# A second DRAIN on GpSimd, placed between the output stores of the last two experts

## The chip, the cores and the metric

The kernel runs on one core of one Trainium2 chip. The metric is device time in microseconds for one execution, and the number that counts is the median over several executions. Time before: 370.25 us, median of 3 runs (368.98 to 373.83).

## What is computed

A gated linear attention over 4 batches, 8 heads, 768 steps and head size 48 gives 3072 tokens of width 384. A mixture of 8 experts then takes them: each expert gets exactly 3072 / 8 = 384 tokens by a greedy assignment on the logits, and each token's output row is one expert's two-layer network.

```python
for t in range(S):
    state = alpha[:, :, t, :, None] * state + np.einsum('bhd,bhe->bhde', k[:, :, t], v[:, :, t])
    y[:, :, t] = np.einsum('bhd,bhde->bhe', q[:, :, t], state)
...
logits = x @ w_gate                     # x: the tokens, 3072 x 384
...                                     # greedy choice, 384 tokens to each expert
for e in range(E):
    mask = assigned == e
    h = np.maximum(x[mask] @ w1[e], 0.0)
    out[mask] = h @ w2[e]
```

## The kernel before

The first 100 us or so are the attention, in 24 units of 128 steps. Then the experts follow one another, `i` = 0 to 7. An expert's 384 tokens are three blocks of 128, `b` = 0 to 2 (`NB` = 3), and its hidden width of 1024 is eight blocks of 128, `q` = 0 to 7 (`FB` = 8), whose weights come in four groups `g` (`GP` = 4). For each `q`, `ffn1` makes the hidden block (`h`, then `hh` and `hl`, its rounded part and the rest), and `ffn2` two blocks later adds its share to the three outputs `y`, one PSUM bank for each token block. Numbers are carried as a high and a low part, so each product is three matmuls.

GpSimd (POOL) issues nearly all transfers of this stage: the gather of an expert's tokens (`xr`, line 1125), the loads of its weights (`wset` and `raw`, lines 1164 and 1178), the loads that add the exact weight onto its negated high part (`wset`, line 1208), and the stores of the output (`out_dram`, line 1335). A store is an indirect DMA that scatters 128 rows of 384 numbers to the tokens' places. Ahead of each stands a small MEMSET of `pcol` (line 1334).

The stores are numbered by `c = i * NB + b`, so that store 20 is the last of expert 6, and 21, 22 and 23 are those of expert 7, the last. Store `c` waits for the eviction of its bank from PSUM to `yo` (ScalarE on line 1326, and for store 23 half of it by VectorE on line 1329). For the last expert the last four `q` are worked through one token block after another (`LAST_BLOCKS` = 4), so that its three outputs are ready one after another and not all at the end.

The order on each engine is fixed while the program is built: every piece of work is an `op(engine, duration, function, after=..., at=...)` and `plan` places them by a list schedule with these durations. What really makes an instruction wait on the chip are the semaphores that the framework derives from the tiles, not the durations or `after`.

When all work is placed, the framework ends the program (line 1413): SyncE waits in turn for the last count of each semaphore, then every engine runs a DRAIN and reports, GpSimd collects the reports and releases all, the semaphores are cleared, and a second such round ends the span. At the start of the program (line 1379) there is one round of the same kind. These are the only DRAINs of GpSimd before the change: one at the start, three in the end.

Of the kernel before, what the change touches and what calls it, by code (L numbers as in the profile page):

```python
# [29 lines left out]
SUBS, SINGLES, WHOLE = (1, 1), 2, 0  # L30
HL_Q = ((0,) * 8, (0,) * 8)
BY_DVE = ((0, 1), (0,))
XL_PE = 1
LB = (0.15, 0.4, 0.7)
LC, LX, LR = (0.15, 0.25, 0.4), (0.15, 0.3, 0.6), (0.15, 0.4, 0.5)
FIRST_HI, FIRST_SP = (1, 1, 2), 0
# [6 lines left out]
def gla_moe_kernel(ctx, tc, q, k, v, alpha, w_gate, w12, out):  # L43
# [10 lines left out]
    E = w_gate.shape[1]  # L54
# [145 lines left out]
    def op(eng, dur, fn, r=(), w=(), banks=(), at=0.0, after=(), lat=LAT, take=None, give=None, follow=(), boost=0.0,  # L200
           dma=0.0, soft=(), small=False, shape=None, ahead=0.12,
           clear=None, until=None, again=LAT):
        o = Op()
        o.small, o.shape, o.ahead, o.clear, o.until, o.again = small, shape, ahead, clear, until, again
        o.take, o.give, o.follow, o.boost, o.dma, o.soft = take, give, follow, boost, dma, soft
        o.eng, o.dur, o.fn, o.banks, o.at, o.lat = eng, dur, fn, banks, at, lat
        o.idx = len(ops)
        pre = set(after)
        for key in r:
            pre |= set(lastw[key])  # L210
            users.setdefault(key, []).append(o)
        for key in w:
            nm, ver = key
            old = (nm, ver - RING.get(nm, 1))
            pre |= set(users.get(old, ())) | set(lastw.get(old, ()))
            lastw.setdefault(key, []).append(o)
        o.pre = pre
        ops.append(o)
        return o
# [64 lines left out]
    V, G, A, P_ = nc.vector, nc.gpsimd, nc.scalar, nc.tensor  # L284
# [448 lines left out]
    for n in range(Y_EARLY, Y_IN_ATTENTION):  # L733
        o = sps[n % 2].rearrange("p a b -> p (a b)")
        xo = None
        for h in range(2):
            xo = op("PE", 0.2, shape=128, fn=lambda n=n, h=h, o=o: (turn_out(n, o, 2 * h), turn_out(n, o, 2 * h + 1)),
                    r=[("yt", n)], after=[*lastw["sm", NU - 1], *([xo] if h else [])], banks=(f"S{n % 2}",), at=40.0 + n,
# [6 lines left out]
    for _ in range(FILLS):  # L745
# [4 lines left out]
        after=lastw["sm", NU - 1] + lates, at=40.0)  # L750
# [13 lines left out]
    GP = FB // 2  # L764
# [36 lines left out]
    def start(i):  # L801
        return F0 + TE * i
# [335 lines left out]
    his, accs, late_w = {}, {}, []  # L1138
# [89 lines left out]
    def prep(i):  # L1228
# [3 lines left out]
        for b in range(NB):  # L1232
# [3 lines left out]
            def ob(b=b, own=own):  # L1236
                bank = YB[b] if own else X2 if b == 1 else XB
                return bank[:, :DB * 128].rearrange("p (d t) -> p d t", d=DB)
# [3 lines left out]
            def tr(b=b, ob=ob):  # L1242
                for d in range(DB):
                    P_.matmul(ob()[:, d], XR[r2][:, b, d * 128:(d + 1) * 128], ident, is_transpose=True, start=d == 0,
                              stop=d == DB - 1 and i >= XL_PE, skip_group_check=True)

# [4 lines left out]
                    w=[("xh", i)], at=at, lat=0.1)  # L1251
            if i < XL_PE:
                x = op("PE", 0.2, lambda ob=ob, bs=bs: P_.matmul(
# [14 lines left out]
    def pe(d_, fn, after, at, **kw):  # L1268
        pe_last[0] = op("PE", d_, fn, after=list(after) + ([pe_last[0]] if pe_last[0] else []), at=at, **kw)
        first_pe.append(pe_last[0])  # L1270
        return pe_last[0]
# [32 lines left out]
    def ffn2(i, qs):  # L1304
        for b in range(NB):
            bs = slice(b * 128, (b + 1) * 128)
            for q in qs:
                n_ = i * FB + q
                g = q // 2
                c0 = (2 + q % 2) * Dm  # L1310

                def fn(n, q=q, b=b, bs=bs, g=g, c0=c0, m=n_ % RX):
                    hi, lo = (WS[i % 2][:, j, g, c0:c0 + Dm] for j in range(2))
                    a, w = ((HHT[m], hi), (HHT[m], lo), (HLT[m], hi))[n]
                    P_.matmul(YB[b][:, :Dm], a[:, bs], w, start=q == 0 and n == 0, stop=q == FB - 1 and n == 2)  # L1315

                for n in range(3):
                    y = pe(0.1735, lambda n=n, fn=fn: fn(n), [(his, accs, his)[n][i, g, 1]],
                           start(i) + (q + 2) * TE / FB,
                           r=[("hl" if n == 2 else "hh", n_), ("wl1" if n == 1 else "wh1", i * GP + g)],  # L1320
                           w=[(f"yb{b}", i)] if q == 0 and n == 0 else [], lat=0.25)
            if FB - 1 in qs:
                c = i * NB + b
                at = start(i) + (FB + 2) * TE / FB
                cut = Dm // 2 if c == E * NB - 1 else Dm
                xs_ = [op("ACT", 0.49, lambda b=b, c=c, cut=cut: A.activation(YO[c % 5][:, :cut], YB[b][:, :cut], AF.Copy),  # L1326
                          after=[y], w=[("yo", c)], at=at, boost=25, lat=0.1)]
                if cut < Dm:
                    xs_.append(op("DVE", 0.3, lambda b=b, c=c, cut=cut: V.tensor_copy(YO[c % 5][:, cut:], YB[b][:, cut:Dm]),
                                  after=[y], w=[("yo", c)], at=at))  # L1330
                users.setdefault((f"yb{b}", i), []).extend(xs_)

                def scatter(b=b, c=c):
                    G.memset(pcol, 0.0)
                    st_ = nc.gpsimd.indirect_dma_start(  # L1335
                        out=out, out_offset=bass.IndirectOffsetOnAxis(ap=IDX[i][:, b:b + 1], axis=0),
                        in_=YO[c % 5], in_offset=None)
                    for other in scattered:
                        tc.declare_no_dep(st_.ins, other.ins, reason="every token's row is stored once")
                    scattered.append(st_)  # L1340

                op("POOL", 1.27, scatter, after=xs_, r=[("yo", c)], at=at + 1, dma=1.2)

    x = None
    for n in range(E * FB + 2):
        i, q = divmod(n, FB)
        if i < E:
            if q == 0:
                if i < NR:
                    x = round_(i, x)  # L1350
                else:
                    last(i, *x)
            if i == 0 and q % 2 == 0:
                ffn1(i, q, (0, 1))
                ffn1(i, q + 1, (0, 1))
            ffn1(i, q, (0, 1, 2) if i else (2,))
        if n >= 2:
            i, q = divmod(n - 2, FB)
            if i < E - 1 or q < FB - LAST_BLOCKS:
                ffn2(i, [q])  # L1360
            elif q == FB - 1:
                ffn2(i, list(range(FB - LAST_BLOCKS, FB)))
# [54 lines left out]
```

## Time and profile before

| | |
|---|---|
| median of 3 runs | 370.25 us (368.98 to 373.83) |
| the profiled execution | 369.01 us |
| its span, first to last instruction | 367.4 us |
| TensorE busy | 350.3 us, 95% |
| VectorE busy | 267.0 us, 73% |
| ScalarE busy | 185.8 us, 51% |
| GpSimd busy | 177.9 us, 48% |
| share of software (GpSimd) queue in DMA time | 54.2% of 16 engines' span |

The profiled execution takes 1.6 us more than its span, and is at the lower end of the runs shown. A DRAIN counts as work of an engine's sequencer, not as busy time, so none of it is in the busy shares. Names such as POOLq or SPq are the sequencers of GpSimd and SyncE.

### The profile page before, as it was taken

To read this page: it belongs to the slowest core of one execution; us is meant where nothing else is said; L and a number is where in the kernel's file an instruction comes from. 1 tells how busy PE (TensorE), PEld (TensorE's weight loads), DVE (VectorE), ACT (ScalarE), POOL (GpSimd) and SP (SyncE) were. 2 spreads that over 40 slices of the span, in tenths; PEclk is the share of its full clock that TensorE was granted. 3 is DMA by queue.
4 is the path that set the end of the run, shared out by engine and by line. 5 is a ranking of instruction groups with operands and counts; after the bars stand their busy time and mean duration, and the time that the engine had idled before them with its cause. 6 is when DMAs were issued, how large, how long until landed. Compare 5 with 4: busy or idle time off the path is not lost.

```text
span 367.4 us, 9669 instructions
## 1 busy us (share of the span) xinstructions
PE 350.3 (95%) x3710; PEld 310.8 (85%) x3710; DVE 267.0 (73%) x741; ACT 185.8 (51%) x387; POOL 177.9 (48%) x298
## 2 busy tenths in 40 slices
PE   8989999999999999899999999999999999999990
PEld 4778888887776779789899989889989999999990
DVE  7999999998878998888978978878777733131110
ACT  4697888886551741651552553543462474343120
POOL 2898999999402312351524625603722862304021
PEclk9999999999999999999999999999999999999996
DMA  7999998840176956999799699698898899986001
GB/s 232 368 351 377 394 300 265 272 131 2 45 249 221 324 105 167 306 173 271 245 218 260 206 243 237 206 272 165 277 266 171 297 337 239 287 201 127 24 22 43
DMA packets 28782, 81.71 MB, mean 222 GB/s; under 512 B 3904, under 2 KB 10304, under 8 KB 28736
## 3 DMA queue, kind: packets, MB, share of 16 engines
q0 software_dynamic: 11024, 52.70, 54.2%
q1 hardware_dynamic: 17712, 28.39, 22.7%
q8 instruction: 29, 0.48, 0.5%
q14 instruction: 17, 0.14, 0.1%
HBM read 71.64 MB, written 9.44 MB: 221 GB/s over the span
## 4 chain that ended last, share of the span: by engine, by line
PE 61%; DVE 19%; issue 9%; DMA 3%; POOL 3%; SPq 1%; ACT 1%; POOLq 0%; DVEq 0%; ACTq 0%
PE h L1283 21%; PE y L1315 21%; PE y L541 3%; DVE sc L449 3%; PE xt L882 3%; PE s L495 2%; DVE ga L454 2%; PE h L1135 2%; DVE kh L459 2%; DVE wset L1190 2%; DMA al<-in_alpha_dram 2%; DVE cmp L935 1%; DMA vr<-in_v_dram 1%; POOL out_dram L1335 1%; DVE xl L1259 1%
## 5 line engine op out<-in xcount | busy, mean ns | idle before, releaser
L1315 PE MATMUL y<-wset,hh 128*128 128x384 f32 x384 | 101.7, 342 | 0.0
L1283 PE MATMUL h<-xh,wset 128*128 128x384 f32 x384 | 93.4, 345 | 0.3 <-DVE hl L1298 0.3
L1296 ACT ACTIVATE hh<-h 128x384 fp32r<-128x384 f32 x64 | 31.3, 490 | 93.7 <-PE h L1283 84.3
L1315 PEld LDWEIGHTS y<-wset,hh 128*128 128x128 f32 x384 | 69.2, 188 | 1.0 <-issue 1.0
L1283 PEld LDWEIGHTS h<-xh,wset 128*128 128x128 f32 x384 | 68.1, 188 | 0.8 <-DVE hl L1298 0.6
L1315 PE MATMUL y<-wset,hl 128*128 128x384 f32 x192 | 65.9, 343 | 0.0
L1298 DVE SCALAR_TENSOR_TENSOR hl<-h,hh 128x384 fp32r<-128x384 f32 x64 | 35.3, 554 | 39.6 <-ACT hh L1296 38.9
L1208 POOL DMA_DIRECT2D wset<-in_w_dram x23 | 20.9, 909 | 63.9 <-ACT wset L1204 63.8
L1283 PE MATMUL h<-xl,wset 128*128 128x384 f32 x192 | 47.3, 345 | 0.0
L1335 POOL DMA_INDIRECT out_dram<-yo,idx x24 | 24.9, 1039 | 41.3 <-ACT yo L1326 37.4
L1204 ACT ACTIVATE wset<-wset 128x768 fp32r<-128x768 f32 x46 | 36.6, 840 | 12.6 <-DMA wset<-in_w_dram 12.2
L1125 POOL DMA_INDIRECT xr<-x_dram,idx x24 | 25.4, 1060 | 23.5 <-DVE idx L1121 9.0
L1315 PEld LDWEIGHTS y<-wset,hl 128*128 128x128 f32 x192 | 36.1, 188 | 0.5 <-issue 0.4
L1283 PEld LDWEIGHTS h<-xl,wset 128*128 128x128 f32 x192 | 34.1, 188 | 0.9 <-issue 0.7
L502 POOL TENSOR_SCALAR_AFFINE_SELECT sm<-sm 128x512 f32<-128x512 f32 x48 | 32.2, 693 | 3.2 <-ACT sm L500 2.9
L464 POOL TENSOR_TENSOR qh<-qr,ga 128x512 f32<-128x512 f32 (+1 forms) x25 | 29.8, 1193 | 5.3 <-DVE ga L454 4.3
L454 DVE TENSOR_TENSOR_SCAN ga<-al,d 128x516 f32<-128x516 f32 (+1 forms) x25 | 29.6, 1183 | 1.8
L449 DVE TENSOR_TENSOR_SCAN sc<-al,d 128x516 f32<-128x516 f32 (+1 forms) x25 | 29.3, 1173 | 1.3 <-DMA al<-in_alpha_dram 1.2
L500 ACT ACTIVATE sm<-s 128x512 f32<-128x512 f32 x48 | 26.1, 595 | 7.3 <-PE s L495 6.8
L495 PE MATMUL s<-qh,kh 64*128 64x128 f32 x384 | 27.4, 282 | 1.0 <-POOL qh L464 1.0
L495 PEld LDWEIGHTS s<-qh,kh 64*128 64x128 f32 x384 | 23.6, 189 | 2.4 <-POOL qh L464 2.1
L1178 POOL DMA_DIRECT2D raw<-in_w_dram x9 | 5.2, 580 | 41.4 <-DVE bk L1098 19.0
(218 smaller groups left out, 590.7 us busy)
## 6 DMA issues: line engine op xcount, KB each, us to landing
wset<-in_w_dram POOLq DMA_DIRECT2D x46, 768.0 KB
raw<-in_w_dram POOLq DMA_DIRECT2D x9, 768.0 KB
qr<-in_q_dram SPq DMA_DIRECT2D x24, 256.0 KB, 4.7
kr<-in_k_dram SPq DMA_DIRECT2D x24, 256.0 KB, 4.8
al<-in_alpha_dram SPq DMA_DIRECT2D x23, 258.5 KB, 4.7
vr<-in_v_dram SPq DMA_DIRECT2D x24, 192.0 KB, 4.6
x_dram<-xga SPq DMA_DIRECT2D x8, 384.0 KB, 2.7
x_dram<-xga SPq DMA_DIRECT2D x8, 192.0 KB, 3.3
```

Source lines behind the costliest of these rows:

```text
L449: V.tensor_tensor_scan(sc[:, lo + 1:hi + 1][:, ::-1], a[:, lo + 1:hi + 1][:, ::-1], dps[:, FO + lo:FO + hi][:, ::-1], 1.0, op0=OP.mult, op ...
L454: V.tensor_tensor_scan(ga[:, lo:hi], a[:, lo:hi], dps[:, lo:hi], 1.0, op0=OP.mult, op1=OP.add)
L464: (V if n in Q_DVE else G).tensor_mul(qh[:, ps_], qr[:, ps_], ga[:, lo:hi].rearrange("p (g x) -> p g x", x=C1)[:, :, 1:])
L495: P_.matmul(sps[h][:, p], kh[hs, p], qh[hs, p], start=True, stop=True)
L500: op("ACT", 0.6, lambda h=h: A.activation(sm[:, h], sps[h], AF.Copy), r=[(f"S{h}", n)], w=[("sm", n)], banks=(f"S{h}",), at=n + 0.4)
L502: op("POOL", 0.65, lambda h=h: G.affine_select(sm[:, h], sm[:, h], pattern=[[0, HP], [1, C]], compare_op=OP.is_ge, fill=0.0, base=0, chann ...
L1204: pre.append(op("ACT", 0.84, lambda hs=hs: A.activation(WS[i % 2][:, 1, g][:, hs], WS[i % 2][:, 0, g][:, hs].bitcast(F32), AF.Copy, scale= ...
L1283: P_.matmul(o(), WS[i % 2][:, a, g, c0 + d * 128:c0 + (d + 1) * 128], x[:, d], start=m_ == 0 and d == 0, stop=m_ == 2 and d == DB - 1)
L1296: a_ = op("ACT", 0.49, lambda: A.activation(HHT[m], o(), AF.Relu), after=[y], r=[("hb", n_)], w=[("hh", n_)], at=at, boost=25, lat=0.1)
L1298: op("DVE", 0.474, lambda: V.scalar_tensor_tensor(HLT[m], o(), 0.0, HHT[m], op0=OP.max, op1=OP.subtract), after=[a_], r=[("hb", n_), ("hh" ...
L1315: P_.matmul(YB[b][:, :Dm], a[:, bs], w, start=q == 0 and n == 0, stop=q == FB - 1 and n == 2)
L1335: st_ = nc.gpsimd.indirect_dma_start(out=out, out_offset=bass.IndirectOffsetOnAxis(ap=IDX[i][:, b:b + 1], axis=0), in_=YO[c % 5], in_offse ...
```

## The change

One instruction is added to GpSimd's queue: a DRAIN, directly behind store 20. It stands ahead of the MEMSET of store 21. It waits for no semaphore and raises none, and no other instruction gained or lost a wait. On all five engines the other instructions stand in the same order as before. The duration of 6.0 and the `after` list tell only the planner where to put it: behind store 20 and behind the last adding loads of the last expert's weights, all of which stood ahead of store 20 already.

```diff
-XL_PE = 1
+XL_PE, DRAINED = 1, 20
...
-                op("POOL", 1.27, scatter, after=xs_, r=[("yo", c)], at=at + 1, dma=1.2)
+                stored = op("POOL", 1.27, scatter, after=xs_, r=[("yo", c)], at=at + 1, dma=1.2)
+                if c == DRAINED:
+                    op("POOL", 6.0, lambda: G.drain(), after=[stored, *(accs[E - 1, g, 0] for g in range(GP))], at=at + 2)
```

## Rows read from the trace of the kernel before

**Rows 1.** The page: span; busy time, share and instructions of TensorE.

```profile
span 367.4 us, 9669 instructions
PE 350.3 (95%) x3710; PEld 310.8 (85%) x3710; DVE 267.0 (73%) x741; ACT 185.8 (51%) x387; POOL 177.9 (48%) x298
```

**Rows 2.** Chain that ended last, its last pieces: start us, us, what.

```profile
358.47 1.01 issue
359.47 1.19 POOLq L1413
```

**Rows 3.** Timeline, 352 to 368: start, us, engine, line, operation, [idle before].

```profile
358.33 0.34 PE L1315 MATMUL y<-wset,hl 128*128 128x384 f32 x1
...
359.07 0.36 DVE L1329 COPY yo<-y 128x192 f32<-128x192 f32 x1 [5.53 <-ACT yo L1326]
```

**Rows 4.** Line 1413, 359.4 to 360: duration ns min/median/max, first and last start.

```profile
L1413 DVEq DRAIN  x1: 395/395/395, 359.1 to 359.1; - x1
L1413 POOLq DRAIN  x1: 7103/7103/7103, 359.5 to 359.5; - x1
```

**Rows 5.** Line 1413, 362.2 to 363, SyncE's sequencer.

```profile
L1413 SPq EVENT_SEMAPHORE  x9: 28/28/28, 362.3 to 362.8; - x9
L1413 SPq DRAIN  x2: 7/7/7, 362.9 to 362.9; - x2
```

**Rows 6.** Waits of SyncE from 360.5 on: us in total, times, longest.

```profile
SPq L1413 <- PEq L1413: 4.4, 2, 3.9
SPq L1413 <- DMA out_dram<-yo,idx: 2.3, 1, 2.3
```

**Rows 7.** Line 1413, from 366.6 on, GpSimd's sequencer.

```profile
L1413 POOLq EVENT_SEMAPHORE  x4: 17/17/17, 366.6 to 367.3; - x4
...
L1413 POOLq DRAIN  x2: 46/75/104, 366.8 to 367.1; - x2
```

**Rows 8.** Line 1379, the first us of the program, GpSimd's sequencer.

```profile
L1379 POOLq DRAIN  x1: 184/184/184, 0.5 to 0.5; - x1
```

**Rows 9.** Stretches of the span: busy us (instructions), granted clock, DMA share, GB/s.

```profile
core 0: us, PE busy (x) PEld busy (x) DVE busy (x) ACT busy (x) POOL busy (x), PEclk, DMA share, GB/s
...
360.66:362.30 1.64, 0.00 (x0) 0.00 (x0) 0.00 (x0) 0.00 (x0) 0.01 (x1) 0.50 0.33 120
362.30:366.60 4.30, 0.00 (x0) 0.00 (x0) 0.00 (x0) 0.00 (x0) 0.00 (x0) 0.50 0.00 0
```

**Rows 10.** DMA issues by line and tile: engine, times, KB each; those of GpSimd.

```profile
wset<-in_w_dram POOLq DMA_DIRECT2D x46, 768.0 KB
raw<-in_w_dram POOLq DMA_DIRECT2D x9, 768.0 KB
...
xr<-x_dram,idx POOLq DMA_INDIRECT x24
out_dram<-yo,idx POOLq DMA_INDIRECT x24
...
probe<-in_moe_w_gate_dram,bsel POOLq DMA_INDIRECT x1
```

**Rows 11.** Timeline of GpSimd from 331 on: the last load, stores 18 to 23.

```profile
331.10 0.88 POOL L1208 DMA_DIRECT2D wset<-in_w_dram  x1 [7.39 <-ACT wset L1204]
...
337.76 1.01 POOL L1335 DMA_INDIRECT out_dram<-yo,idx  x1 [0.19 <-issue]
338.77 0.11 POOL L1334 MEMSET pcol<- 128x1 f32 x1
339.07 0.96 POOL L1335 DMA_INDIRECT out_dram<-yo,idx  x1 [0.19 <-issue]
340.02 0.12 POOL L1334 MEMSET pcol<- 128x1 f32 x1
355.31 0.95 POOL L1335 DMA_INDIRECT out_dram<-yo,idx  x1 [15.17 <-ACT yo L1326]
...
357.39 0.96 POOL L1335 DMA_INDIRECT out_dram<-yo,idx  x1 [1.01 <-ACT yo L1326]
...
359.71 0.96 POOL L1335 DMA_INDIRECT out_dram<-yo,idx  x1 [1.24 <-DVE yo L1329]
```

**Rows 12.** Line 1335, the output stores: ns min/median/max, first and last start.

```profile
L1335 POOL DMA_INDIRECT out_dram<-yo,idx x24: 955/1008/1707, 161.9 to 359.7; - x24
```

## Prediction

> **What bounds the kernel now.** I read the page first: TensorE is busy for 350.3 of 367.4 us [rows 1], so the body of the kernel belongs to it, and an instruction on GpSimd can matter only where GpSimd is late or where TensorE has already stopped. The chain that ended last ends on GpSimd's sequencer at the program's closing line, and nothing on it follows [rows 2]. So I read the end in order of time. TensorE's last matmul is over at 358.33 + 0.34 = 358.67, and VectorE's half of the last eviction at 359.07 + 0.36 = 359.43 [rows 3]. The last store is issued from 359.71 to 360.67 [rows 11]. SyncE waits 2.3 us for that store to land, begins the rest of its waits at 362.3, and has done its own drains at 362.9 [rows 5, 6]. Then nothing moves: from 362.30 to 366.60 every engine's busy time is 0.00 and the DMA share is 0.00 [rows 9]. SyncE waits 3.9 us for its release [rows 6]. The row puts that wait down to the sequencer of TensorE, which had long been done. What really is late is GpSimd's DRAIN: it starts at 359.47 and takes 7.10 us, so it ends at 366.57 [rows 2, 4]. The report round starts at 366.6 [rows 7], and the span ends 0.8 us later at 367.4. So the last 3.7 us (366.6 - 362.9) ahead of that round belong to one instruction, the final DRAIN of GpSimd.
>
> **What that DRAIN does.** VectorE's drain ends at 359.1 + 0.4 = 359.5, together with its last instruction at 359.43 [rows 3, 4]. GpSimd's is another matter: it ends 366.57 - 360.67 = 5.90 us after its last issue and 366.57 - 362.3 = 4.27 us after that issue's data has landed [rows 4, 5, 11]. In those 4.27 us no transfer moves, so it isn't waiting for data. It is doing, or waiting for, something of its own. What that grows with can be read from the other three drains of GpSimd. The one at the start, with no transfer issued before it, takes 0.184 us [rows 8]. The two behind the long one, with no transfer in between, take 0.104 and 0.046 us [rows 7]. The long one follows 46 + 9 + 24 + 24 + 1 = 104 transfers that GpSimd has issued since the program began [rows 10]. So a drain's length hangs on transfers that no drain has yet cleared away. Whether it hangs on how many there are, or only on there being any, the trace of before can't show, since there is but one drain with transfers before it.
>
> The two ends of this unknown: if it goes by the number, each of 104 costs 4.27 / 104 = 41 ns to 5.90 / 104 = 57 ns, and a drain behind three transfers has 0.12 to 0.17 us of own work. If it is one fixed job, it takes 4.27 us after the landing however few there are. I take the number. The nearest rows are the stores: they follow each other 337.76, 339.07 on one queue with 0.19 us of idle time between a store and its MEMSET [rows 11], so what one transfer leaves to be done is not of the size of 4 us, or it would have to be put off; a hundred small leftovers put off to the drain add up to it, and one leftover does not. The fixed job stays as a rival.
>
> **The added DRAIN, in its place.** It stands behind store 20, whose issue ends at 339.07 + 0.96 = 340.03 [rows 11]. Ahead of it are 101 of the 104 transfers; the last big one was issued at 331.10 [rows 11]. By the store at the end its data lands 362.3 - 360.67 = 1.6 us after issue, so at 341.6. Then 101 x 41 ns = 4.2 us, or at most 101 x 57 ns = 5.8 us, puts its end between 345.8 and 347.5. Queued behind it are only the MEMSETs and stores 21 to 23 and the program's end, and store 21 can't be issued before its eviction, at 355.31 after 15.17 us of idle time [rows 11]. So 7.8 us of cover remain (355.31 - 347.5), and the added drain costs **nothing**. No engine waits on a semaphore of it. TensorE, VectorE and ScalarE run on as before, since all weights of the last expert are already issued.
>
> If that cover were gone: store 22 has 1.01 us of idle time before it and store 23 has 1.24 us [rows 11], so store 21 could be 1.01 + 1.24 = 2.25 us late before store 23 moved. The drain would have to last until 357.5, that is 17.5 us, 2.5 times the longest one in the trace. From there on each further us costs one us.
>
> **The final DRAIN, after.** It now follows three transfers. It can't end before the last of them is out at 360.67, and if it waits for the landing not before 362.3; with 0.12 to 0.17 us of work it ends at 362.5 at the latest. SyncE's last drain at 362.9 is then later. The report round would start at 362.9 instead of 366.6, so the gain is **3.7 us**: less than the 4.27 us that vanish from the drain, since 0.6 us of SyncE's waits come out from under it. That also bounds the gain from above: a drain of no length at all gives no more, because SyncE sets the end next. From below the bound is 0, for a fixed job.
>
> The sum against the profiled execution: 369.01 + 0 - 3.7 = 365.3 us. The profiled one is at the low end of the runs shown, and their median is 1.2 us above it. I name 365.7, between the sum and the sum with that distance.
>
> **A rule weighed against the trace.** The drain's end at 366.57 stands 4.27 us behind the last landing, with no engine busy in between [rows 4, 5, 9]. The Trainium skill, page "PSUM — Partial Sum Buffer", section "Engine vs sequencer instructions", says that a drain waits for its engine to go fully idle. Taken by itself that rule speaks against this change, since the last store is the same before and after: by it the sum would be 369.0 in place of 365.3. The trace agrees for VectorE; for GpSimd it leaves 4.27 us that the rule doesn't explain.
>
> **Rivals.**
> *One fixed job (no change).* The final drain pays 4.27 us after the landing whenever any transfer came before it. For it: a single long drain can't tell. Against it: the stores' spacing, as above. The added drain is covered all the same, so the time is 369.0, at the runs' median 370.25. Chance 0.14. A relative of it: the work of a drain has to be fetched before it runs, and the stores in between drive it out again. The Trainium skill, page "GPSIMD Engine Reference", section "Instruction dispatch", has some 6 us (5.95) for the first call of newly loaded code, with no instruction to be seen in the profile; the 5.90 us here is close to it, and no run here shows whether that is more than chance.
> *Only what is still running (no change).* The 4.27 us are the completion of the last store alone, in a form that the trace doesn't show; an earlier drain then takes nothing from it. For it: the drain's end is the only sign of when GpSimd is done. Against it: the store's count has reached SyncE by 362.3 and the DMA share is 0.00 from there on [rows 5, 9]. The time is again 369.0. Chance 0.06. It is what the rule of "PSUM — Partial Sum Buffer" in the Trainium skill would make of this kernel.
> *In part.* The work goes with something of which the last three stores hold a larger share than 3 in 104 (rows, or time since the transfer), and the final drain ends between 362.9 and 366.57. Halfway gives 367.2. Chance 0.06.
> *Slower.* The added drain outlasts its cover, say because each earlier transfer costs more than the final drain shows. Place: the gap ahead of store 21. It decides from 17.5 us on; at 20 us the last store is 2.5 us late. Then the time is 369.01 + 2.5 = 371.5 if the final drain keeps its length, 367.8 if it doesn't. Also under this: the first store after the drain is dearer. The dearest store in the trace takes 1.707 us against a median of 1.008 [rows 12], and 0.7 us more disappears in the 1.01 us of idle time before store 22. Chance 0.03.
> *The forecast:* 0.71.
>
> **How the numbers follow.** Predicted 365.7. The forecast's own range is 364.6 (0.7 below the sum, since executions differ by tenths and nothing in the rows gives more than 3.7) to 366.9 (1.6 above the sum). The partial case and the near part of the two no-change cases reach up to 369.5; what lies beyond it, their rest and the slower case, is about 0.15. So 364.6 to 369.5. About 2%, 7.4 us, is what a measurement of this kernel can tell from no change. The whole gain is half of that, so it should come out as within 2%: 0.93. Faster by over 2% needs a gain of twice what the end of the program holds, or scatter of the runs on top: 0.05. Slower by over 2% needs an added drain of 17.5 + 7.4 = 24.9 us: 0.02.
>
> **What would show each step.** A DRAIN of POOLq on a new line starts near 340.0 and lasts 5.8 to 7.5 us: the leftover goes by number and lies under cover. Store 21 still starts near 355.3: cover holds. The first of the closing drains of POOLq falls from 7.10 to about 3 us (ending with the landing) or 1.4 us (not waiting for it), SyncE's longest wait at the closing line falls from 3.9 us to about 0.2, and the span becomes 363.7. Wrong, by the fixed job: the closing drain still takes about 7.1 us although the added one took as long. Wrong, by the slower rival: store 21 waits for the drain and not for its eviction. A short added drain, under 2 us, with a long final one would say that neither number nor presence of earlier transfers is what it pays for.

## The result, and the profile after

The changed kernel takes 366.34 us (median of 6 runs, 364.96 to 367.59); the kernel before, measured beside it, 370.08 us (6 runs, 368.98 to 373.83). The medians differ by 3.7 us. The ratio is 0.9892, with a 95% interval of 0.9856 to 0.9929, which is 4.0 us less, between 2.6 and 5.3. So the gain is within 2%, and it is clear of no change.

The page of the changed kernel has one instruction more, and a body that is no shorter; TensorE's busy time is 351.0 us, against 350.3 [rows 1].

```profile
span 365.6 us, 9670 instructions
PE 351.0 (96%) x3710; PEld 311.3 (85%) x3710; DVE 267.6 (73%) x741; ACT 185.9 (51%) x387; POOL 178.3 (49%) x298
```

The sequencers' instructions on the new line (1344) and on the closing line (now 1415), with their least, median and longest duration in ns and the start of the first and the last:

```profile
L1344 POOLq DRAIN  x1: 7667/7667/7667, 340.0 to 340.0; - x1
...
L1415 POOLq DRAIN  x3: 46/104/2963, 361.4 to 365.3; - x3
L1415 SPq DRAIN  x3: 7/7/7, 364.7 to 365.1; - x3
```

The added DRAIN lasts 7.67 us, and the first closing one has gone from 7.10 to 2.96 us [rows 4]. SyncE's waits at the closing line, in total, times and longest:

```profile
SPq L1415 <- PEq L1415: 0.7, 2, 0.5
```

It was 4.4 us, 3.9 the longest [rows 6]. The 0.5 us that is now the longest is the second of the two waits, which before was 4.4 - 3.9 = 0.5 as well; the first is down to 0.2. The timeline of GpSimd, with idle time in brackets, answers to [rows 11]:

```profile
339.66 1.01 POOL L1335 DMA_INDIRECT out_dram<-yo,idx  x1 [0.18 <-issue]
340.67 0.11 POOL L1334 MEMSET pcol<- 128x1 f32 x1
340.98 0.96 POOL L1335 DMA_INDIRECT out_dram<-yo,idx  x1 [0.19 <-issue]
347.78 0.10 POOL L1334 MEMSET pcol<- 128x1 f32 x1 [5.84 <-issue]
357.21 0.95 POOL L1335 DMA_INDIRECT out_dram<-yo,idx  x1 [9.34 <-ACT yo L1326]
358.16 0.12 POOL L1334 MEMSET pcol<- 128x1 f32 x1
359.29 0.96 POOL L1335 DMA_INDIRECT out_dram<-yo,idx  x1 [1.01 <-ACT yo L1326]
360.25 0.11 POOL L1334 MEMSET pcol<- 128x1 f32 x1
361.61 0.96 POOL L1335 DMA_INDIRECT out_dram<-yo,idx  x1 [1.24 <-DVE yo L1329]
```

The MEMSET of store 21 now waits 5.84 us behind the drain, and store 21 still waits for its eviction, with 9.34 us to spare. Stores 22 and 23 follow as before, with the same 1.01 and 1.24 us of idle time.

The span of this execution is only 1.8 us shorter (365.6 against 367.4), though the end of the program, from the end of the last issue, has gone from 367.4 - 360.67 = 6.7 us to 365.6 - 362.57 = 3.0 us. The difference of 1.9 us was there before the drain was reached: store 19 starts at 339.66 where it started at 337.76 [rows 11]. Executions of one kernel differ by that much: the spans of the six timed ones run from 363.3 to 365.9 us.

### The profile page after: what moved, and what is told of

The parts are those of the page before. It is cut to its first block, busy times and chain, and to the rows that moved or that the text cites. A ratio compares the mean times of both kernels' runs of the same rounds, so it can differ in the third digit from the quotient of the medians.

```text
span 365.6 us, 9670 instructions
## 1 busy us (share of the span) xinstructions
PE 351.0 (96%) x3710; PEld 311.3 (85%) x3710; DVE 267.6 (73%) x741; ACT 185.9 (51%) x387; POOL 178.3 (49%) x298
## 4 chain that ended last, share of the span: by engine, by line
PE 50%; DVE 18%; issue 13%; DMA 10%; POOL 5%; ACT 2%; POOLq 1%; SPq 1%; DVEq 0%; ACTq 0%
PE h L1283 16%; PE y L1315 16%; DMA wset<-in_w_dram 5%; PE y L541 3%; DVE sc L449 3%; PE s L495 3%; DVE ga L454 3%; DVE kh L459 2%; DMA raw<-in_w_dram 2%; PE xt L882 2%; DMA al<-in_alpha_dram 2%; DVE wset L1190 1%; POOL out_dram L1335 1%; PE xt L1244 1%; PE h L1135 1%
```

## Experiments

The kernels stand on the kernel before, and only the last on the changed one. A DRAIN behind a store is put in by hand inside `scatter`, unseen by the planner, so that the order of all other work stays as it was. What is compared is the drains themselves and the end of the program, since the rest varies by some 2 us from one execution to the next. Landings are the last of the 16 counts that a store adds to its semaphore in the trace.

**One drain early, behind store 2.**

```diff
                     scattered.append(st_)
+                    if c == 2:
+                        G.drain()
```

> The added DRAIN stands behind store 2 (end of expert 0) and nowhere else; 23 transfers ahead of it, 81 behind it. By number of transfers (57 ns each, counted from the end of the last issue): the added drain has 1.3 us of work, less than the 1.6 us its last store needs to land, so it ends 1.6 to 1.9 us behind that issue; the final drain ends 81 x 57 ns = 4.6 us behind the last issue (before: 5.9), and the end of the program, from the last issue to the span's end, is 5.4 us (before 6.7, changed kernel 3.0). Once only (the first drain behind any transfer pays some 5.8 us, later ones find it done): the added drain takes 5.8 us, the final one ends about 1.8 us behind the last issue, the end of the program is 3.0 us.

The added DRAIN and the closing ones:

```profile
L1342 POOLq DRAIN  x1: 11751/11751/11751, 163.7 to 163.7; - x1
...
L1415 POOLq DRAIN  x3: 52/104/7883, 366.3 to 374.7; - x3
```

"Once only" is out: the final drain is 7.88 us long, although one with 23 transfers went before. But the count as I had it is wrong in two ways. The final drain ends 5.09 us behind the last landing, where 81 transfers at 41 ns give 3.3, and 6.69 us behind the last issue, where 57 ns give 4.6. And the added drain lasts 11.75 us and ends 9.9 us behind the issue of store 2, where 1.6 to 1.9 was expected. The stretch from the store's issue to its landing, in busy time, clock, DMA share and GB/s, shows why:

```profile
164.70:174.40 9.70, 9.70 (x73) 9.07 (x72) 8.13 (x36) 1.48 (x3) 0.87 (x1) 1.00 0.81 195
174.40:175.40 1.00, 1.00 (x18) 0.84 (x16) 0.41 (x4) 0.00 (x0) 0.00 (x0) 1.00 0.00 0
```

Store 2 lands only at 174.4, 8.9 us behind its issue, in a stretch in which the DMA engines are 81% busy: the two loads of weights issued just ahead of the stores, at 159.29 and 160.78, land at 169.3 and 173.0. The drain waits for store 2, and then works 1.0 us more. So a drain of GpSimd waits for all that GpSimd has in flight. Meanwhile nothing else can be issued from GpSimd's queue:

```profile
176.75 0.57 POOL L1178 DMA_DIRECT2D raw<-in_w_dram  x1 [11.18 <-DVE nd L964]
```

In the kernel before this load is issued at 169.78. Here it starts 1.3 us behind the end of the drain (175.43), which is what it waited for, and not the instruction of VectorE that the row names. The weights of a later expert come 7.0 us late, and the last store is issued at 367.48 instead of 360.67. One execution took 376.63 us.

**Three drains, behind stores 2, 11 and 20.** The same edit with `if c in (2, 11, 20)`.

> Three added DRAINs, behind stores 2, 11 and 20, with 23, 40 and 38 transfers between them and 3 behind the last. By number: 1.3, 2.3 and 2.2 us of work, so they end 1.6 to 1.9, 2.3 and 2.2 us behind the issue ahead of each (together about 6 us where the changed kernel's one drain has 5.8); the final one ends with the landing, 1.8 us behind the last issue. Once only: 5.8 us for the first, about 1.8 us for the second, third and last. One fixed job per drain: about 5.8 us for each of the four.

```profile
L1342 POOLq DRAIN  x3: 5094/6535/11107, 162.8 to 347.4; - x3
...
L1415 POOLq DRAIN  x3: 46/104/2950, 368.8 to 372.7; - x3
```

From the landing ahead of each, the three work 0.99 us (23 transfers), 1.69 us (40) and 1.60 us (38), and the final one 0.16 us (3). That is neither one fixed job nor one paid once: it is the number, at 41 ns each, counted from the landing and not from the issue. The 57 ns of the prediction's other end would be 2.3 and 2.2 us from the issue; they are 4.60 and 3.21. The end of the program is 3.04 us long, as in the changed kernel, but the first two drains have no cover, and the last issue ends at 369.96. One execution took 374.61 us.

**A drain before any transfer.** In the kernel before, at the end of the attention:

```diff
+    def first_transfer():
+        G.drain()
+        nc.gpsimd.indirect_dma_start(out=probe, ...)
-    op("POOL", 1.2, lambda: nc.gpsimd.indirect_dma_start(
+    op("POOL", 1.2, first_transfer, ...)
```

> The kernel before with one DRAIN ahead of GpSimd's very first transfer, behind all of its work in the attention. By number of transfers: that drain takes under 0.4 us, the final one again 5.9 us behind the last issue, the time that of before. By number of GpSimd's instructions of all kinds (298, so 20 ns each): that drain takes about 3.5 us beyond the end of the work ahead of it, and the final one ends some 2.3 us behind the last issue. A first call that has to be fetched: several us here, and the final one as long as it likes.

The drain, and from the timeline GpSimd's last work ahead of it:

```profile
L749 POOLq DRAIN  x1: 897/897/897, 94.5 to 94.5; - x1
```

```profile
94.02 1.27 POOL L502 TENSOR_SCALAR_AFFINE_SELECT sm<-sm 128x512 f32<-128x512 f32 x2 [0.32 <-ACT sm L500]
```

It lasts 0.90 us, more than the 0.4 that were expected, because its record starts while the work ahead of it still runs. It ends at 94.48 + 0.90 = 95.37, 0.08 us behind that work (95.29). GpSimd's instructions as such leave nothing to a drain, nor does the first drain in the body cost a fetch of several us. The final one is again 7.10 us long and ends 4.30 us behind the landing. One execution took 368.82 us.

**24 small transfers more.** The kernel before, with 24 loads of 32 bytes behind the first transfer:

```diff
+    tiny = [rw.tile([1, E], F32, name=f"tiny{j}") for j in range(24)]
...
+        for t in tiny:
+            nc.gpsimd.dma_start(t, w_gate[:1])
```

> The kernel before, no added DRAIN, with 24 more transfers of 32 bytes each behind GpSimd's first transfer, in the gap between the attention and the experts (their data is not used). By number: 128 transfers x 57 ns = 7.3 us from the last issue to the end of the final drain (before 5.9), the end of the program 8.1 us, the time 1.4 us above before. By rows or bytes: 24 x 1 row on top of 104 x 128 rows, so 5.9 us and the time of before.

```profile
L1419 POOLq DRAIN  x3: 46/110/8086, 360.9 to 369.5; - x3
```

The final drain is 8.09 us long, 0.98 us more, and ends 5.28 us behind the landing. 0.98 / 24 = 41 ns for a transfer of one row and 32 bytes, the same as for the 104 others (4.30 / 104), most of which are far larger. Number counts, rows and bytes don't. The end of the program is 7.7 us, not 8.1: the 57 ns were too high. One execution took 371.37 us.

**Behind store 2 once more, and behind store 11.** The kernel of the first run again, and `if c == 11`.

> The kernel of the first of these runs once more (one added DRAIN, behind store 2), since its final drain was longer than the rest of the runs would have it: 5.09 us behind the last landing for 81 transfers, where 23, 38, 40, 101, 104 and 128 transfers all fit 0.05 us + 41 ns each. By that line: 3.4 us behind the last landing. If something of the order of transfers since a drain counts beside their number: again 5.1 us.

> One added DRAIN, behind store 11, with 63 transfers ahead of it and 41 behind. By 0.05 us + 41 ns for each transfer, counted from the last landing: the added drain ends 2.6 us behind the landing of store 11, the final one 1.7 us behind that of store 23. If the final drain after an early one is dearer (as behind store 2, with a surplus of 1.7 us): 2.5 us or more for the final one. Once only: final 0.2 us.

```profile
L1415 POOLq DRAIN  x3: 52/104/7885, 366.7 to 375.1; - x3
```

The surplus behind store 2 comes back to the hundredth: 5.09 us behind the landing for 81 transfers. With the drain behind store 11, the added one takes 2.63 us behind the landing, as expected (2.6), and the final one 1.82 us, 0.09 above the 1.73 that 0.05 us + 41 ns each would give. One execution each took 377.04 and 373.43 us.

**Where the surplus comes from: behind the first transfer, store 5 and store 8.** The edits `if c == 5` and `if c == 8`, and a drain right behind the first transfer of all.

> One added DRAIN right behind GpSimd's very first transfer, in the gap between the attention and the experts: 1 transfer ahead of it, 103 behind it. By 0.05 us + 41 ns each: it ends 0.1 us behind the landing of that transfer, and the final drain 4.3 us behind the last landing, so the time is that of before. If in a later batch the transfers beyond the 40th cost twice as much (which would fit 5.09 us for 81 and 1.82 us for 41): 4.3 + 63 x 41 ns = 6.9 us behind the last landing, 2.6 us slower than before. If any earlier drain makes the final one 1.7 us dearer: 6.0 us.

> One added DRAIN, behind store 5 (end of expert 1): 36 transfers ahead of it, 68 behind. It waits for store 5 to land and then works 1.5 us. The final drain, behind the last landing: 2.8 us by the number alone; 4.0 us if those beyond the 40th of a later batch cost twice as much; 4.5 us if an earlier drain costs 1.7 us.

> One added DRAIN, behind store 8 (end of expert 2): 50 transfers ahead of it, 54 behind. It waits for store 8 to land and then works 2.1 us. The final drain, behind the last landing: 2.3 us by the number alone; 2.8 us if those beyond the 40th of a later batch cost twice as much; 4.0 us if an earlier drain costs 1.7 us.

One execution each took 370.57, 376.78 and 375.86 us. The drains that had transfers to clear away (left out are nine that repeat a row within 0.01 us, or 102 transfers with 4.22), with the time from the last landing to their end, and what 0.05 us + 41 ns for each transfer gives:

| kernel | transfers since the drain before | behind the landing, us | line, us |
|---|---|---|---|
| first transfer: added | 1 | 0.09 | 0.09 |
| store 22: final | 1 | 0.09 | 0.09 |
| changed: final | 3 | 0.17 | 0.17 |
| store 2: added | 23 | 0.99 | 0.99 |
| store 5: added | 36 | 1.53 | 1.53 |
| three drains: third | 38 | 1.60 | 1.61 |
| three drains: second | 40 | 1.69 | 1.69 |
| store 8: added | 50 | 2.10 | 2.10 |
| store 11: added | 63 | 2.63 | 2.63 |
| changed: added | 101 | 4.18 | 4.19 |
| store 22: added | 103 | 4.26 | 4.27 |
| before: final | 104 | 4.30 | 4.31 |
| 24 small: final | 128 | 5.28 | 5.30 |
| first transfer: final | 103 | 4.26 | 4.27 |
| store 11: final | 41 | 1.82 | 1.73 |
| store 8: final | 54 | 2.89 | 2.26 |
| store 5: final | 68 | 4.02 | 2.84 |
| store 2: final | 81 | 5.09 | 3.37 |

Fourteen rows lie on the line within 0.02 us. The line was drawn after those of 3, 23, 38, 40, 101, 104 and 128 transfers; those of 1, 36, 50, 63 and 103 were measured afterwards. The last four lie above it by 0.09, 0.63, 1.18 and 1.72 us, in steps of about 41 ns for each transfer beyond the 39th or 40th. "Any earlier drain makes the final one 1.7 us dearer" is out by the first three of them. "Those beyond the 40th of a later batch cost twice" fits all four (2.8 and 4.0 were expected for stores 8 and 5), and falls with the drain behind the first transfer, whose later batch of 103 has no surplus. The two batches always add up to 104, so the surplus of the four can as well hang on how many came before the first drain; the drain behind the first transfer fits that no better. The cause stays open. It does not touch the change, whose last drain has three transfers and lies on the line.

**A drain without cover, behind store 22.** `if c == 22`, in 10 runs against 13 of the kernel before.

> One added DRAIN with no cover: behind store 22, with only store 23 behind it. The drain waits 1.6 us for store 22 to land and then works 103 x 41 ns + 0.05 = 4.3 us, so it ends some 5.9 us behind the issue of store 22, when the last eviction has long been done; store 23 is issued 0.3 us later. In the times of the kernel before: 358.35 + 5.9 + 0.3 = 364.55, issued by 365.5, landed by 367.1, SyncE done by 367.75, the span's end at 368.5, so 1.1 us slower than before (ratio 1.003) and 4.8 us slower than the changed kernel. The final drain is as short as in the changed kernel, 0.1 to 0.2 us behind the landing. If a drain under way doesn't hold the store back: the time of the changed kernel, ratio 0.990.

The ratio is 1.0054, with an interval of 1.0028 to 1.008: 2.0 us slower (1.0 to 3.0), where 1.1 was expected. The timeline of GpSimd:

```profile
358.26 0.96 POOL L1335 DMA_INDIRECT out_dram<-yo,idx  x1 [1.01 <-ACT yo L1326]
365.14 0.10 POOL L1334 MEMSET pcol<- 128x1 f32 x1 [5.92 <-issue]
365.90 0.96 POOL L1335 DMA_INDIRECT out_dram<-yo,idx  x1 [0.66 <-issue]
```

The drain ends 5.85 us behind store 22, as expected (5.9), and it does hold back store 23. That store is issued not 0.3 but 0.8 us behind the drain's end (365.08 to 365.90), so the profile's own sum is 1.6 us: from the start of store 22 to that of store 23 it is 5.3 us longer than before (7.64 against 2.32), and the shorter final drain gives 3.7 us of it back. In the other runs, too, a DMA that had only the drain to wait for started well behind the drain's end: 0.73 us behind store 11 and 1.33 us behind store 2. The same instruction, two stores later, turns 1.1% gained into 0.5% lost.

**One small transfer more in the changed kernel.** GpSimd's transfers count on eight semaphores in turn, and SyncE waits for them in a fixed order at the end. One more transfer moves the last store to another semaphore.

```diff
+    tiny = [rw.tile([1, E], F32, name=f"tiny{j}") for j in range(1)]
...
+        for t in tiny:
+            nc.gpsimd.dma_start(t, w_gate[:1])
```

> The changed kernel with one more small transfer (32 bytes, not used) behind GpSimd's first one, so that the last store counts on another of the eight semaphores that GpSimd's transfers share in turn; SyncE reaches that one as the seventh of its closing waits and no longer as the second. If SyncE's row of waits sets the end (0.63 us from the landing to its last drain): from the landing to SyncE's last drain 0.3 us, from the last issue to the span's end 2.7 us in place of 3.04. If the final drain of GpSimd sets it: 3.04 as before.

```profile
L1422 SPq EVENT_SEMAPHORE  x12: 17/28/2007, 357.3 to 362.8; - x12
L1422 POOLq DRAIN  x3: 46/110/2958, 358.9 to 362.5; - x3
L1422 SPq DRAIN  x3: 7/7/7, 361.9 to 362.2; - x3
```

The last store lands at 361.70, and SyncE's drains are done at 362.0, 0.3 us later instead of 0.63. From the last issue to the span's end it takes 2.71 us, as expected. So it is SyncE that sets the end of the changed kernel.

> The changed kernel with one more small transfer, as looked at before, now timed against the kernel before. The changed kernel stands at 0.989 of the kernel before; the end of the program is 0.33 us shorter still, 0.09%, so 0.988, a step too small for the interval to tell from the changed kernel.

It takes 366.71 us (4 runs, 365.32 to 367.74) against 371.45; the ratio is 0.987, with an interval of 0.981 to 0.993. That beats the kernel before, and can't be told from the changed kernel.

## Why the prediction was right, point by point

**What sets the end.** Right. The final DRAIN of GpSimd was what the last 3.7 us belonged to: with it shortened, the end of the program from the last issue on is 3.7 us shorter (6.7 to 3.0), and the time, by the ratio, 4.0 us (2.6 to 5.3), against a forecast of 3.7.

**Number, or one fixed job.** Right that it goes by the number. The profile after alone would have allowed a job that is paid once, by whichever drain comes first. The drain behind store 2 shut that out, since the final one stayed long, and the 24 small transfers shut out rows and bytes. The argument from the stores' spacing pointed the right way, but was no proof.

**The size.** Of the two ends, 41 ns from the landing and 57 ns from the issue, the first is right: fourteen drains of 1 to 128 transfers fit it within 0.02 us, with 0.05 us on top of each. The four with a surplus don't, but none of them is in the changed kernel. A drain first waits for the last landing and only then works off its list. In the changed kernel's profile this can be seen at the added drain: the stretch from the end of store 20's issue to its landing, and from there to the drain's end, with busy times, clock, DMA share and GB/s.

```profile
341.94:343.53 1.59, 1.59 (x11) 1.59 (x10) 0.00 (x0) 0.19 (x1) 0.00 (x0) 1.00 0.34 124
343.53:347.71 4.18, 4.18 (x26) 4.18 (x25) 1.11 (x2) 0.79 (x2) 0.00 (x0) 1.00 0.02 4
```

4.18 us for 101 transfers, with the DMA engines at 2%.

**The added drain under cover.** Right. It ends 5.77 us behind store 20's issue, at the early end of what was given (345.8 to 347.5, with the issue ending at 340.03). The late end was a slip: it counted from the landing the 57 ns that had been worked out from the issue. Counted from the issue they give 345.8 as well. (The 101 x 41 ns are 4.1 us, not 4.2.) The length of the DRAIN, 7.67 us, is just outside the 5.8 to 7.5 named as a sign, since its record starts at 340.04, 1.9 us ahead of the end of store 20's issue. Store 21 still had 9.34 us of idle time ahead of it (forecast: at least 7.8).

**SyncE is next.** Right: the gain stops at SyncE's waits, 0.63 us behind the landing. The end of the changed kernel, in the same columns:

```profile
362.57:364.17 1.60, 0.00 (x0) 0.00 (x0) 0.00 (x0) 0.00 (x0) 0.00 (x0) 1.00 0.34 123
364.17:364.80 0.63, 0.00 (x0) 0.00 (x0) 0.00 (x0) 0.00 (x0) 0.00 (x0) 1.00 0.00 0
```

By the line, 14 transfers behind the added drain would still fit into those 0.63 us (0.05 + 14 x 0.041 = 0.62).

**The rivals.** The fixed job, and only what is still running, are both out: behind the same last store the final drain ended 4.30 us after the landing, or 0.17. The partial case is out with them, since 0.17 us is what three transfers give by the line. So is work that stores drive out and that must be fetched again: three stores stand between the added drain and the final one. The rule in the Trainium skill, page "PSUM — Partial Sum Buffer", section "Engine vs sequencer instructions", that a drain waits for its engine to go fully idle, fits the drain ahead of any transfer, which ended 0.08 us behind the engine's last work. It leaves out both the wait for the landing and the work on the list: in the two rows above, of 1.59 and 4.18 us, GpSimd's busy time is 0.00. The price of lost cover had its mechanism right: behind store 22, what the drain lasted beyond the gap held up the last store. But the bound of 17.5 us counted the idle times of stores 22 and 23 whole, though 0.19 us stay between a MEMSET and its store [rows 11], and it was set against the longest drain of the trace, which stands at the quiet end of the program. Where weights are in flight, a drain with only 23 transfers on its list took 10.6 to 11.8 us.

**What was chosen.** 365.7 was named, between the sum of 365.3 and the sum with the median's distance; the measured median is 366.34, and the kernel before stood at 370.08 beside it. The difference was forecast better than the level. The 0.4 us that 365.7 adds to the sum was a choice, and the low end of the range rested on executions that differ by tenths, while the six of the changed kernel lie 2.6 us apart and those of the kernel before 4.9. So it is partly luck that the median came out within 0.7 us of 365.7; the end of the program, 3.7 us shorter in the traces, is what bears the prediction out.

## What to carry to other kernels

Look at what the last instruction to finish is waiting for, also when it belongs to the program's closing rounds and not to any line of work: here 1% of the time lay behind the last store, with every engine and the DMA idle. If a cost grows with what has piled up, pay it earlier, where the engine waits anyway, and leave to the end only what the next thing in line hides. Place it where nothing large is in flight and the wait behind it is longer than the cost: the same drain gained 4.0 us behind store 20, lost 2.0 us behind store 22, and held up the issue of weights by 7 us behind store 2.

## What the runs showed of the hardware

A DRAIN on GpSimd waits until all transfers that GpSimd has issued have landed (behind store 2, which took 8.9 us to land, it lasted 11.75 us). Then it takes 0.05 us and 41 ns for each transfer since the drain before (0.09 us for 1, 0.99 for 23, 4.30 for 104), whatever their size: 24 transfers of 32 bytes added 0.98 us. With no transfer it ended 0.08 us behind the engine's last work. In four kernels with a single added drain, behind store 2, 5, 8 or 11, the final drain took 0.09 to 1.72 us more than that; why is open.
